# The second pair's first layer in two-level form, and its block sums spread over three earlier places

## The chip, the cores and the metric

The kernel runs on one core of a Trainium2 chip. Its time is the device time of one execution in microseconds (us). The core has five engines that run side by side, each with its own instruction queue that is worked off in order: TensorE (PE in the profile, with its weight loads as PEld), VectorE (DVE), ScalarE (ACT), GpSimd (POOL) and SyncE (SP), which here only issues DMAs. ScalarE and GpSimd issue some DMAs too. An instruction that waits on a semaphore holds all that stands behind it in its queue.

## The reference, cut to what matters

Four batches of 768 rows and 512 columns (8 heads of 64) go through a decayed linear attention in blocks, then through a Fourier mixing layer, a layer norm and an MLP:

```
attn_out = lightning attention of q, k, v with a decay per head
x    = attn_out as (4, 768, 512)
u    = x + real(fft over rows and columns of x)
un   = (u - mean(u)) / sqrt(var(u) + 1e-06)
out  = u + maximum(un @ w_ch1, 0) @ w_ch2
```

`w_ch1` is 512 x 2048 and `w_ch2` is 2048 x 512, all in float32. The MLP is what the change is about.

## The kernel before, in words

**Units of work.** The rows of a batch are cut into six tiles of 128 rows; a group is two of them, so that there are 12 groups of 256 rows. The first four groups (`PLAIN`) go through the MLP with ordinary matrix products (`mlp`), woven between the attention and the Fourier mixing of the four batches. The last eight (`LATE`) make four pairs, numbered 0 to 3, which are done at the end (`late`). For these the normalised rows were put into DRAM (`utd`), transposed, and so were the rows `u` (`ud`).

**Seven products in place of eight.** In a pair, both layers multiply blocks by a scheme that needs seven products of half-size blocks where the plain way needs eight; in exchange, sums and differences of the blocks of both operands are formed ahead (`combine_weights` makes those of the weights, once: `s1` to `s4` of `w_ch1` and `t1` to `t4` of `w_ch2`), and the results are added up from the accumulators. `PRODUCTS` lists the seven, 0 to 6, by their operand names. Two-level means that each of the seven is itself done by seven products of quarter blocks (`seven`), for which sums of the quarters are needed: three of them are read from DRAM (`load_three`), the fourth (the difference S3) takes the place of a quarter of the weight block itself.

**What the pairs do.** The second layer is two-level in all four pairs (`second_layer`, `deep_second`; matmuls on line 1048). The first layer is one-level in pairs 0 and 1 (`first_layer`, matmuls on line 893, 128 x 256) and two-level in pairs 2 and 3 (`deep_first`, matmuls on line 978, 128 x 128). `DEEP = 2` says so. The order of products in a two-level first layer is `FIRST = [0, 3, 4, 2, 1, 5, 6]`.

**Who makes the quarter sums.** Those of `w_ch2` (`keep_sums`, line 731, to DRAM as `td`) are made by GpSimd during pair 0's first layer, those of `w_ch1` (`keep_sums_w`, line 747, as `sd`) by GpSimd during pair 1's first layer: seven blocks of four sums each, 128 x 512, with the results written to DRAM through the SP queue. After that `place_sums_w` writes the seven S3 into the weight blocks (line 753).

**Order around the change.** The program is recorded once and a scheduler orders every engine's instructions when it is built, some of them pinned to the order of the text. In a second layer and a two-level first layer, `in_step` runs two neighbouring products alternately; the loads of the next product's sums (line 770, six buffers `tx`, three per product) and the sums of the activations stand in front of it. Each of the seven steps in a product is added into a PSUM accumulator, which VectorE or ScalarE reads (`read`, lines 1054 and 1056 in the second layer, 985 and 987 in the first) before the step after next adds to it again: the first, third, fifth and seventh step share one accumulator. The sums of the activations are made by VectorE: lines 872, 874 and 876 (`prepare_a`), 858 (`split`) and 950 (`part_sum`). The input rows of a pair come by `load_u` (line 759) into the buffer `ur`, of which there is one. The results of a pair lie in the tile `y2`, of which there is one too; it is stored by two SP DMAs (line 631) and two GpSimd scatter DMAs (line 633). GpSimd also adds `u` to the results (line 1062).

**The last batch's attention.** A batch is worked off in six chunks of 128 rows. In each, VectorE multiplies two tiles of scores by the decay (line 304) that TensorE made (line 300) and that it uses next (line 341); GpSimd makes `kd` (line 272) and the decayed state (line 324), and starts the gathers of mirrored rows (lines 448, 454 and 461).

Of the kernel before, what the change touches and what calls it, by code (L numbers as in the profile page):

```python
# [10 lines left out]
F32 = mybir.dt.float32  # L11
# [65 lines left out]
def kernel(  # L77
# [162 lines left out]
                yield 1.0  # L240


    xs, xn_, xd = {}, {}, {}

    def pair(t, hp):
# [45 lines left out]
    def attn_out(b, c, head):  # L291
        kT, qT, qs, kd, vt = ins.pop((b, c))
        last = c == NC - 1


        mm = nc.tensor.matmul
        pss = [psum_a([C, HP, C]) for _ in range(2)]
        for hp in range(HP):
            for hi in range(2):
                mm(pss[hi][:, hp, :], lhsT=kT[HD[hi], hp, :], rhs=qT[HD[hi], hp, :], start=True, stop=True)  # L300
        sc = []
        for hi in range(2):
# [12 lines left out]
        if not last:  # L315
            pu = psum_a([128, HP, D])
            for hp in range(HP):
                for hi in range(2):
                    h = 2 * hp + hi
                    mm(pu[HD[hi], hp, :], lhsT=kd[:, h, :], rhs=vt[:, h, :], start=True, stop=True)  # L320
            if c == 0:
                nc.vector.tensor_copy(s_new, pu)
            else:
                nc.gpsimd.tensor_tensor(s_new, s_old, spow.broadcast_to([128, HP, D]), op=ALU.mult)
                nc.vector.tensor_tensor(s_new, s_new, pu, op=ALU.add)
            if not padded:
                yield 0.9


        po = psum_a([128, HP, C])  # L330
        if c > 0:
            for hp in range(HP):
                for hi in range(2):
                    old, qh = (sd[:, hp, hi, :], qs[:, hp, :]) if padded else (s_old[HD[hi], hp, :], qs[HD[hi], hp, :])
                    mm(po[HD[hi], hp, :], lhsT=old, rhs=qh, start=(hp == 0), stop=False, skip_group_check=True)  # L335
        if padded and not last:
            for hi in range(2):
                nc.scalar.copy(sd[HD[hi], :, hi, :], st[HD[hi]])
        for hp in range(HP):
            for hi in (1, 0) if padded else (0, 1):  # L340
                mm(po[HD[hi], hp, :], lhsT=vt[:, 2 * hp + hi, :], rhs=sc[hi][:, hp, :],  # L341
                   start=(c == 0 and hp == 0), stop=(hp == HP - 1), skip_group_check=True)
        oT = new(at, [128, HP, C], "oT")
        nc.scalar.copy(oT, po)
        if b in TURNED:

            if c == 0:
                nc.scalar.copy(first, po[:, :, 0:1])
            elif c > 1:
                nc.scalar.copy(oTs[b][:, :, 0:1], po[:, :, 0:1])  # L350
        yield 2.0
        yield from head

        def turn(oT):
            px = psum_a([C, HP, 128])
            for hp in range(HP):
                nc.tensor.transpose(px[:, hp, :], oT[:, hp, :], ident)  # L357
            return px.rearrange("p h e -> p (h e)")

        def put(px, x, n=128):  # L360
            nc.scalar.copy(x[0:n, 0:HM], px[0:n, 0:HM])
            nc.scalar.copy(x[0:n, HM:DM], px[0:n, DM - 1:HM - 1:-1])

        def back(oT, x):
            put(turn(oT), x)

        if b not in TURNED:
            x = xn_[b, c] = new(xp, [C, DM], "x") if c < HC else new(xn, [C, DM], "xn")
            back(oT, x)
            if c == 0:  # L370
                xd[b] = (dram.tile([S - 256, DM], F32, name=f"xa{b}"), dram.tile([257, DM], F32, name=f"xb{b}"))
                nc.scalar.dma_start(xd[b][1][256:257], x[0:1])
            elif not last:
                nc.scalar.dma_start(xd[b][0][(c - 1) * C:c * C], x)
            if c >= NC - 2:
                nc.scalar.dma_start(xd[b][1][(c - NC + 2) * C:(c - NC + 3) * C], x)
            if c == NC - 2 and b - 1 not in LEADS:
                mirror_a(b)
            elif last:
                mirror_b(b)  # L380
            yield 1.7
            return


        if c == 2:
            eo[b] = new_eo()

        def mirrored(m, px):
            if m < HC:
                put(px, eo[b][HC - 1 - m][1][:, 1, 0:DM][0:BLK[HC - 1 - m]], BLK[HC - 1 - m])  # L390
            else:
                u = xs[b, HC + NC - 1 - m] = new(xp, [128, DM], "x")
                put(px, u)

        px = turn(oTs[b]) if c > 1 else None
        if c > 0:

            oTs[b] = new(fp, [128, DM + 4], "ds")[:, 0:DM].rearrange("p (h c) -> p h c", h=HP)
            tc.keep_in_program_order(nc.scalar.copy(oTs[b][:, :, C - 1:0:-1], po[:, :, 1:C]))
        if last:  # L400
            tc.keep_in_program_order(nc.scalar.copy(oTs[b][:, :, 0:1], first))
        if c > 1:
            mirrored(c - 1, px)
            yield 1.4
        if not last:
            x = xn_[b, c] = new(xp, [C, DM], "x") if c < HC else new(xn, [C, DM], "xn")
            back(oT, x)
            yield 1.7
        else:
            mirrored(c, turn(oTs[b]))  # L410
            for t in range(HC):
                xs[b, t] = xn_.pop((b, t))
            yield 1.4
# [317 lines left out]
            pin(nc.gpsimd.tensor_tensor(o, x, y, op=op))  # L731
            nc.sync.dma_start(s2.td[k][i], o)

    s2.sd = []

    def quarters_w(t):

        return [t[:, k, f:f + FH // 2] for f in (0, FH // 2) for k in range(2)]

    def keep_sums_w(k):  # L740

        pin = tc.keep_in_program_order
        A11, A12, A21, A22 = quarters_w(s2.A[PRODUCTS[k][0]])
        S3, S2, S1, S4 = [new(s2.yp, [128, FH // 2], "tx", bufs=6) for _ in range(4)]
        s2.sd.append([dram.tile([128, FH // 2], F32, name=f"sd{k}{i}") for i in range(4)])
        for i, o, x, y, op in ((3, S3, A11, A21, SUB), (1, S2, A22, S3, SUB), (0, S1, S2, A11, ADD), (2, S4, A12, S2, SUB)):
            pin(nc.gpsimd.tensor_tensor(o, x, y, op=op))
            nc.sync.dma_start(s2.sd[k][i], o)

    def place_sums_w():  # L750

        for k, (a, _) in enumerate(PRODUCTS):
            nc.sync.dma_start(quarters_w(s2.A[a])[2], s2.sd[k][3])

    def load_u(j, queue=nc.sync):

# [18 lines left out]
        pass  # L775

    PAIRS = len(LATE) // 2
    DEEP = 2
    pairs = [Pair() for _ in range(PAIRS)]
    for P_ in pairs:  # L780
        P_.pre_a, P_.pre_b, P_.pre_w = {}, {}, {}
# [104 lines left out]
    def first_layer(j):  # L886
# [24 lines left out]
        for i in range(HF):  # L911
# [14 lines left out]
            V.tensor_tensor(a22, two(Z), a22, op=ADD)  # L926
            V.tensor_scalar(a22, a22, 0.0, None, op0=ALU.max)
            last = (i, X, Z)
            if j < min(DEEP, 2) and i < len(PRODUCTS):
                if i == 0:  # L930
                    tc.keep_in_program_order(nc.gpsimd.tensor_copy(s2.begun, h["a11"][:, 0, 0, 0:1]))
                (keep_sums, keep_sums_w)[j](i)
            if i == HF - 3:
                load_x(j)
            if i == HF - 2:
# [4 lines left out]
        run(prepare_a(j, 0))  # L940
        finish(*last)
        run(prepare_a(j, 1))
        if j + 1 < PAIRS:
            load_u(j + 1)
        open_y(j)

    def part_sum(e, o, x, y, op):
# [17 lines left out]
    def deep_first(j, k):  # L965
# [15 lines left out]
        def read(ps, r, s, first):  # L981
# [7 lines left out]
            if k > 3 and done[r, s] == (1 if (r, s) == (0, 1) else 2):  # L989
                nc.scalar.activation(o, o, AF.Relu)  # L990

        yield from seven(mm, read)

        T, a11, a12, a21, a22 = (h[n] for n in ("s1", "a11", "a12", "s3", "a22"))
# [37 lines left out]
    def deep_second(j, k):  # L1032
# [18 lines left out]
        def read(ps, s, m, first):  # L1051
# [3 lines left out]
            else:  # L1055
                V.tensor_tensor(o, ps[:, 0:HM // 2], o, op=ADD)  # L1056

        yield from seven(mm, read)

        def add_u(o, y, k, m):  # L1060
# [19 lines left out]
        elif k == 3:  # L1080
            V.tensor_tensor(y22, y22, T, op=ADD)
            add_u(y21, y22, 1, 0)
            add_u(T, T, 0, 1)
            add_u(y22, y22, 1, 1)
        elif k == 4:
            V.tensor_tensor(y22, y22, y12, op=ADD)
            V.tensor_tensor(y12, y12, T, op=ADD)
        elif k == 5:
            store(*who[1][1], yt[:, 1, 1])
        else:  # L1090
            store(*who[0][1], yt[:, 0, 1])
            store(*who[1][0], yt[:, 1, 0])
            store(*who[0][0], yt[:, 0, 0])
# [54 lines left out]
                        del live[q]  # L1148

    def late():  # L1150
        for j in range(PAIRS):
            if j < DEEP:
                open_pair(j)
                if j == 0:
                    run(inputs(0))
                first_layer(j)
                if j + 1 < DEEP:
                    in_step(second_layer(j) + [(inputs(j + 1), iter(()))])
        in_step(second_layer(DEEP - 1) + [w for j in range(DEEP, PAIRS) for w in deep_pair(j)])


# [113 lines left out]
```

## Time and profile before

| | us |
|---|---|
| median of three runs | 793.12 |
| lowest and highest run | 791.16 and 796.66 |
| the profiled execution's own time | 794.64 |
| its span, from the first to the last instruction | 792.3 |
| TensorE busy in the span | 763.7 (96%) |
| weight loads | 648.6 (82%) |
| VectorE | 587.0 (74%) |
| ScalarE | 224.9 (28%) |
| GpSimd | 196.2 (25%) |

All instants below are us from the start of the span. The stages of the end, by the lines of TensorE's matmuls: pair 0's first layer from 427, its second layer from 472; pair 1's first layer from 518, its second layer from 564; pair 2 from 607 with a two-level first layer, pair 3 from 695. TensorE's busy time counts modelled ends, so that a busy row says that it was not waiting, not that it could go no faster. The granted TensorE clock was 0.994 of full speed in the mean.

### The profile page before, as it was taken

How to read it: one execution, taken by the hardware profiler on the slowest of the kernel's cores; microseconds unless marked ns; L12 is line 12 of the kernel's file. 1: busy time of each engine (PE TensorE's matmuls, PEld its weight loads, DVE VectorE, ACT ScalarE, POOL GpSimd, SP SyncE). 2: the span in 40 equal slices, each digit the busy share in tenths (PEclk: the TensorE clock that was granted, in tenths of full speed). 3: DMA queues.
4: the chain of work that ended last, by engine and by line, in shares of the span. 5: the costliest groups of instructions: out<-in, count | busy, mean ns of one | idle time of the engine just before them, and what ended most of it. 6: DMA issues, size and time to landing. Idle time of an engine off the chain costs nothing.

```text
span 792.3 us, 14623 instructions
## 1 busy us (share of the span) xinstructions
PE 763.7 (96%) x5616; PEld 648.6 (82%) x5616; DVE 587.0 (74%) x1148; ACT 224.9 (28%) x532; POOL 196.2 (25%) x198
## 2 busy tenths in 40 slices
PE   6889989999999899999999999999999999999996
PEld 5768776858675876868946889988999999999996
DVE  6899889675745482345698998769966699758983
ACT  3665443335531221421201221022211342024300
POOL 3213331011111020211003960279204001230012
PEclk9999999999999899999999999999999999999999
DMA  9979724238843138431243375345954555456442
GB/s 236 258 155 249 194 81 127 96 62 213 218 125 99 40 59 167 120 99 43 54 120 104 136 244 158 98 167 193 346 151 148 160 175 182 126 174 186 132 121 81
DMA packets 152331, 116.80 MB, mean 147 GB/s; under 512 B 113998, under 2 KB 113998, under 8 KB 152262
## 3 DMA queue, kind: packets, MB, share of 16 engines
q1 hardware_dynamic: 147120, 103.39, 46.7%
q0 software_dynamic: 2112, 6.69, 2.6%
q10 hardware_dynamic: 3030, 5.78, 2.0%
q8 instruction: 45, 0.74, 0.4%
q14 instruction: 24, 0.20, 0.1%
HBM read 83.58 MB, written 32.25 MB: 146 GB/s over the span
## 4 chain that ended last, share of the span: by engine, by line
PE 81%; DVE 9%; DMA 4%; issue 2%; ACT 1%; POOL 1%; POOLq 0%; SPq 0%; ACTq 0%
PE p L1048 21%; PE p L893 12%; PE p L978 11%; PE pm L658 10%; PE pm L644 10%; PE pa L525 3%; PE pa L300 3%; PE pa L341 3%; DMA x<-xb,ix 2%; PE pa L335 2%; PE pa L276 1%; PE pa L320 1%; PE pa L281 1%; PE pa L357 1%; DVE sc L304 1%
## 5 line engine op out<-in xcount | busy, mean ns | idle before, releaser
L644 PE MATMUL pm<-ut,w 128*128 128x256 f32 x512 | 118.4, 381 | 0.0
L658 PE MATMUL pm<-w,hr 128*128 128x512 f32 x256 | 115.3, 596 | 0.1
L644 PEld LDWEIGHTS pm<-ut,w 128*128 128x128 f32 x512 | 94.5, 190 | 13.6 <-issue 2.1
L658 PEld LDWEIGHTS pm<-w,hr 128*128 128x128 f32 x256 | 46.7, 190 | 50.3 <-issue 48.9
L1062 POOL TENSOR_TENSOR y<-y,u 128x512 f32<-128x512 f32 x12 | 18.9, 1572 | 199.1 <-DVE y L1071 156.7
L1048 PE MATMUL p<-tx,sx 128*128 128x128 f32 x416 | 54.9, 275 | 0.0
L1048 PEld LDWEIGHTS p<-tx,sx 128*128 128x128 f32 x416 | 50.6, 192 | 0.0
L272 POOL TENSOR_TENSOR kd<-k,decay 128x512 f32<-128x512 f32 x20 | 22.5, 1124 | 97.9 <-PE pa L320 51.6
L893 PE MATMUL p<-ur,w 128*128 128x256 f32 x192 | 46.7, 379 | 0.0
L1054 ACT COPY y<-p 128x128 f32<-128x128 f32 x48 | 12.8, 266 | 104.1 <-PE p L1048 103.1
L1056 DVE TENSOR_TENSOR y<-p,y 128x128 f32<-128x128 f32 x92 | 25.5, 285 | 22.5 <-PE p L1048 15.9
L893 PEld LDWEIGHTS p<-ur,w 128*128 128x128 f32 x192 | 36.4, 190 | 5.3 <-issue 0.5
L1048 PE MATMUL p<-w,ha 128*128 128x128 f32 x288 | 37.4, 275 | 0.0
L300 PEld LDWEIGHTS pa<-qT,kT 64*128 64x128 f32 x384 | 26.1, 193 | 13.0 <-ACT qT L283 7.8
L304 DVE TENSOR_TENSOR sc<-pa,decay 128x512 f32<-128x512 f32 x48 | 31.4, 682 | 6.6 <-PE pa L300 6.4
L1048 PEld LDWEIGHTS p<-w,ha 128*128 128x128 f32 x288 | 35.0, 192 | 0.2
L652 ACT ACTIVATE hr<-pm 128x256 f32<-128x256 f32 x44 | 16.7, 385 | 63.8 <-PE pm L644 63.6
L300 PE MATMUL pa<-qT,kT 64*128 64x128 f32 x384 | 30.7, 292 | 3.4 <-ACT qT L283 3.1
L558 POOL TENSOR_SCALAR ve<-mv 128x2 f32<-128x2 f32 x12 | 3.3, 278 | 121.8 <-DVE mv L555 121.8
L893 PE MATMUL p<-sx,w1s 128*128 128x256 f32 x128 | 32.9, 380 | 0.5 <-DVE sx L796 0.5
L341 PE MATMUL pa<-sc,v 128*64 128x128 f32 x384 | 29.9, 279 | 2.8 <-DVE sc L304 2.8
L987 DVE TENSOR_TENSOR ha<-p,ha 128x512 f32<-128x512 f32 x40 | 26.7, 684 | 6.5 <-PE p L978 6.3
(234 smaller groups left out, 1723.1 us busy)
## 6 DMA issues: line engine op xcount, KB each, us to landing
tx<-td SPq DMA_DIRECT2D x84, 256.0 KB, 2.9
raw<-in_moe_w_ch_dram SPq DMA_DIRECT2D x32, 512.0 KB, 4.8
tx<-sd SPq DMA_DIRECT2D x42, 256.0 KB, 2.8
sd<-tx SPq DMA_DIRECT2D x28, 256.0 KB, 2.0
k<-in_k_dram SPq DMA_DIRECT2D x24, 256.0 KB, 5.5
q<-in_q_dram SPq DMA_DIRECT2D x24, 256.0 KB, 5.1
v<-in_v_dram SPq DMA_DIRECT2D x24, 256.0 KB, 4.5
td<-tx SPq DMA_DIRECT2D x21, 256.0 KB, 2.0
```

The lines of the kernel that those rows point to most:

```text
L272: nc.gpsimd.tensor_tensor(kd, kt, kpow, op=ALU.mult)
L300: mm(pss[hi][:, hp, :], lhsT=kT[HD[hi], hp, :], rhs=qT[HD[hi], hp, :], start=True, stop=True)
L304: nc.vector.tensor_tensor(t, pss[hi], decay[:, hi::2, :], op=ALU.mult)
L341: mm(po[HD[hi], hp, :], lhsT=vt[:, 2 * hp + hi, :], rhs=sc[hi][:, hp, :], start=(c == 0 and hp == 0), stop=(hp == HP - 1), skip_group_chec ...
L525: mm = nc.tensor.matmul(ps[:, n, :], lhsT=piece(a, i, n), rhs=cs[0:rows, a, i in (2, 3), n, :], start=(a == 0), stop=(a == 1))
L644: nc.tensor.matmul(ps, lhsT=w1[:, c, 128 * fc:128 * fc + 128], rhs=ut[:, c, :], start=(c == 0), stop=(c == KO - 1))
L658: nc.tensor.matmul(ps, lhsT=hr[(fc - f0) // 4][:, fc % 4, 128 * i:128 * i + 128], rhs=w2[:, fc, :], start=(fc == f0), stop=(fc == f1 - 1))
L893: nc.tensor.matmul(ps, lhsT=s2.A[a][:, kt, 128 * i:128 * i + 128], rhs=U[b][:, kt, :], start=(first and kt == 0), stop=(kt == 1), skip_gro ...
L978: nc.tensor.matmul(ps[:, 128 * i:128 * i + 128], lhsT=ab[m][0][:, 128 * i:128 * i + 128], rhs=ab[m][1], start=(start and i == 0), stop=Tru ...
L987: V.tensor_tensor(o, p, o, op=ADD)
L1048: nc.tensor.matmul(ps[:, 0:HM // 2], lhsT=ab[m][0][i], rhs=ab[m][1][:, i, :], start=(start and i == 0), stop=(i == HF // 2 - 1), skip_grou ...
L1056: V.tensor_tensor(o, ps[:, 0:HM // 2], o, op=ADD)
```

## The change

`DEEP` goes from 2 to 1, so that pair 1's first layer is two-level as well. Its sums of `w_ch1` quarters must then be there before pair 1, and they are made by one new function, `block_sums`, in three places:

- for products 0, 1 and 5 by VectorE in chunks 1 to 4 of the last batch's attention, one of the twelve sums at each `next(early)`, in two buffers of the pool `ep`; all four results of a block go to DRAM by the GpSimd queue;
- for products 3 and 4 by GpSimd at the start of pair 0's second layer, in a spare `ur` buffer; S3 is formed in place in the weight block, the three others go to DRAM by the GpSimd queue;
- for products 2 and 6 by GpSimd at the start of pair 1's first layer, in a spare `y2` buffer; S3 in place, the three others go to DRAM by the SP queue.

`place_sums_w` now writes three S3 and runs in pair 0's second layer. The load of pair 1's rows (`load_u(1)`) moves from the end of pair 0's first layer to the fourth product of its second layer. The 28 sums of `keep_sums_w` and their DMAs in pair 1's first layer go.

```diff
+    def quarters_w(t):
+        return [t[:, k, f:f + DFF // 4] for f in (0, DFF // 4) for k in range(2)]
+    sums_of = {}
+    def block_sums(eng, queue, k, t, stage, inside):
+        Q11, Q12, Q21, Q22 = quarters_w(t)
+        d = sums_of[k] = [dram.tile([128, DFF // 4], F32, name=f"sd{k}{i}") for i in range(4)]
+        s1, s2_, s4, s3 = (stage[i] for i in range(4))
+        o = {3: Q21 if inside else s3, 1: s2_, 0: s1, 2: s4}
+        for i, x, y, op in ((3, Q11, Q21, ALU.subtract), (1, Q22, 3, ALU.subtract), (0, 1, Q11, ALU.add), (2, Q12, 1, ALU.subtract)):
+            x, y = (o[z] if isinstance(z, int) else z for z in (x, y))
+            tc.keep_in_program_order(eng.tensor_tensor(o[i], x, y, op=op))
+            if i < 3 or not inside:
+                queue.dma_start(d[i], o[i])
+            yield 1.0
+    def front_sums():
+        for k, a in ((0, w1[:, 0:2, 0:DFF // 2]), (1, w1[:, 2:4, 0:DFF // 2]), (5, w1[:, 2:4, DFF // 2:DFF])):
+            E, F = (new(ep, [128, DFF // 4], "e") for _ in range(2))
+            yield from block_sums(nc.vector, nc.gpsimd, k, a, (E, F, F, E), False)
+    early = front_sums()
...
+        sums = b == B - 1 and 0 < c < NC - 1
+        if sums:
+            next(early)
         po = psum_a([128, HP, C])
...
         nc.scalar.copy(oT, po)
+        if sums:
+            next(early)
...
+            if sums:
+                next(early)
             if c == NC - 2 and b - 1 not in LEADS:
...
-    def keep_sums_w(k):
...
-        for k, (a, _) in enumerate(PRODUCTS):
-            nc.sync.dma_start(quarters_w(s2.A[a])[2], s2.sd[k][3])
+        for k in (0, 1, 5):
+            nc.sync.dma_start(quarters_w(s2.A[PRODUCTS[k][0]])[2], s2.sd[k][3])
...
-    DEEP = 2
+    DEEP = 1
...
-            if j < min(DEEP, 2) and i < len(PRODUCTS):
+            if i < len(PRODUCTS):
...
-                (keep_sums, keep_sums_w)[j](i)
+                keep_sums(i)
...
         run(prepare_a(j, 1))
-        if j + 1 < PAIRS:
-            load_u(j + 1)
         open_y(j)
...
+        if j == DEEP and k < 2:
+            if k == 0:
+                P.spare = spare_y()
+            run(block_sums(nc.gpsimd, nc.sync, (2, 6)[k], s2.A[("s3", "s4")[k]], P.spare, True))
         yield from seven(mm, read)
...
+        if j < DEEP and k < 2:
+            if k == 0:
+                P.spare = spare_u()
+            run(block_sums(nc.gpsimd, nc.gpsimd, (3, 4)[k], s2.A[("s2", "s1")[k]], P.spare, True))
         yield from seven(mm, read)
...
             add_u(y22, y22, 1, 1)
+            if j < DEEP:
+                load_u(j + 1)
...
     def late():
-        for j in range(PAIRS):
-            if j < DEEP:
-                open_pair(j)
-                if j == 0:
-                    run(inputs(0))
-                first_layer(j)
-                if j + 1 < DEEP:
-                    in_step(second_layer(j) + [(inputs(j + 1), iter(()))])
+        open_pair(0)
+        run(inputs(0))
+        first_layer(0)
         in_step(second_layer(DEEP - 1) + [w for j in range(DEEP, PAIRS) for w in deep_pair(j)])
```

In this cut, the first `if` stands at the start of a product of `deep_first` and the second at the start of one of `deep_second`. In the program as built, TensorE's order is the same as before up to pair 0's last products; VectorE's is the same but for the twelve sums in the attention and for pair 1. In the SP queue, the two DMAs of `load_u(1)` stand between the first and the second of the three loads for pair 0's product 3 (counted from 0), and the six writes of the sums of products 2 and 6 stand among the loads of pair 1's products.

More of the change, by code (lines that the diff above doesn't have):

```diff
@@ L732, in keep_sums, with four, spare_u, spare_y @@
             nc.sync.dma_start(s2.td[k][i], o)
-    s2.sd = []
-    def quarters_w(t):
-        return [t[:, k, f:f + FH // 2] for f in (0, FH // 2) for k in range(2)]
-    def keep_sums_w(k):
[L742 to L748, printed above, removed]
+    s2.sd = sums_of
+    def four(t):
+        return [t[:, 512 * i:512 * i + 512] for i in range(4)]
+    def spare_u():
+        return four(new(s2.up, [128, 2, KO, G * 128], "ur").rearrange("p a b c -> p (a b c)"))
+    def spare_y():
+        return four(new(s2.yp, [128, 2, G, DM], "y2").rearrange("p a b c -> p (a b c)"))
     def place_sums_w():
-        for k, (a, _) in enumerate(PRODUCTS):
-            nc.sync.dma_start(quarters_w(s2.A[a])[2], s2.sd[k][3])
+        for k in (0, 1, 5):
+            nc.sync.dma_start(quarters_w(s2.A[PRODUCTS[k][0]])[2], s2.sd[k][3])
     def load_u(j, queue=nc.sync):
```

## The prediction

> **What bounds the kernel now.** I read the page's slices first, then the chain that ended last, then the stretches, and last the time order of single instructions where two engines meet. The slices (40 of 19.8 us each) show TensorE at eight or nine tenths from the second slice on. GpSimd is full only in slices 23 and 28, in the two one-level first layers, and there VectorE is at nine too.
>
> ```profile
> PE   6889989999999899999999999999999999999996
> ...
> DVE  6899889675745482345698998769966699758983
> ...
> POOL 3213331011111020211003960279204001230012
> ```
>
> The chain, in order of time (start, length, what), is TensorE alone from 427 to 780:
>
> ```profile
> 427.21 45.13 PE p L893 x208
> 472.34 0.67 PE p L1048 x6
> 473.01 1.79 PE p L893 x8
> 474.80 43.10 PE p L1048 x386
> 517.90 46.62 PE p L893 x216
> 564.52 0.67 PE p L1048 x6
> 565.19 1.79 PE p L893 x8
> 566.98 40.42 PE p L1048 x362
> ```
>
> So a matmul saved at the end is time saved, as long as nothing that feeds TensorE becomes late.
>
> **The gain.** Pair 1's first layer is 224 matmul records on line 893: 46.62 + 1.79 = 48.41 us, 0.216 each. In two-level form it is 7 products x 7 steps x 8 records = 392. Pair 2 has just this, without a gap:
>
> ```profile
> 612.76 38.41 PE p L978 x344
> ```
>
> 38.41 / 344 = 0.1117, and 392 x 0.1117 = 43.77. The gain is **4.64 us**. That the 28 GpSimd sums in pair 1's first layer go (of some 1.35 us each) is worth nothing by itself: TensorE was dense beside them.
>
> **The twelve sums in the attention.** VectorE gets 12 x 0.68 (line 872 has the same operands) = 8.2 us, GpSimd 12 DMA issues; a plain DMA from that queue does not occur before, the nearest row is the scatter on line 633 with 1.06 us of the engine and 3.0 from issue to landing. Between 304 and 347 VectorE has gaps of 8.3, 3.0, 3.0, 3.4, 2.6, 2.6 and 4.3 us, and GpSimd has gaps of 14.7 and 3 us. Most of it lies beside TensorE's work. The catch: with two buffers, a sum waits until an earlier one has landed in DRAM, and behind it in VectorE's queue stand the score products (line 304), which TensorE uses 0.1 us after they end (end 333.24, use from 333.37; 339.12 and 339.25). In chunk 2, the sum ending at 328.45 is written by 328.5 + 3.0 = 331.5, so the one that waits ends at 332.2 where the scores start at 332.03: 0.1 to 0.2 late. In chunk 3 the like count gives 338.0 against 337.91. I take **+0.2**; bounds 0 (landing in 2.0, as SP's writes of `sd`) and 2.5 (4.3, the slowest GpSimd gather's, which adds 1.3 in each of the two chunks). The GpSimd queue is through at 346.2, before the gather at 347.30.
>
> **Sums 3 and 4 in pair 0's second layer: the dear part.** GpSimd was idle there and seems free. VectorE is not:
>
> ```profile
> core 0: us, PE busy (x) PEld busy (x) DVE busy (x) ACT busy (x) POOL busy (x), PEclk, DMA share, GB/s
> 472.00:485.00 13.00, 13.00 (x109) 12.77 (x108) 12.71 (x25) 2.74 (x10) 0.00 (x0) 1.00 0.70 227
> ```
>
> 12.71 of 13 us, with GpSimd at 0.00. And the two hinder each other. Of these lines the first two and the last ran while GpSimd summed, the third while it was idle; the fourth is a read of PSUM that I come to below:
>
> ```profile
> 461.98 1.75 DVE L858 TENSOR_TENSOR ha<-ha 128x512 f32<-128x512 f32 x1
> ...
> 465.27 1.48 DVE L908 TENSOR_TENSOR hs<-ha,sv 128x256 f32<-128x256 f32 x1
> ...
> 468.61 0.68 DVE L858 TENSOR_TENSOR ha<-ha 128x512 f32<-128x512 f32 x1
> ...
> 479.64 0.28 DVE L1056 TENSOR_TENSOR t<-p,t 128x128 f32<-128x128 f32 x1
> ...
> 505.19 1.34 DVE L874 TENSOR_TENSOR sx<-sx,ha 128x512 f32<-128x512 f32 x1
> ```
>
> The same sum of two SBUF operands takes 0.68 alone and up to 1.75 beside GpSimd: up to 1.07 per GpSimd sum. The three GpSimd adds at 503.5 to 507.7 cost VectorE only 0.66 + 0.30, so 0.32 each. Those are the bounds. When: the first sum can start when its weight block is last used (470.5), the second when `ur` is free (473.96, where the load of line 759 got going). From there five sums and three DMA issues take 5 x 1.27 + 3 x 1.06 = 9.5, to 483.5. So six sums start before 482.00, which is when TensorE adds the seventh step of product 0 to an accumulator:
>
> ```profile
> 482.00 1.06 PE L1048 MATMUL p<-w,sx 128*128 128x128 f32 x8
> ```
>
> It may do so once VectorE has read the fifth step, which is the line at 479.64, done at 479.92: 2.1 us to spare. VectorE's queue ahead of that read has no gap from 470 on and is 15 operations on SBUF to 5 that read PSUM, so nearly all that it loses arrives there. Six sums cost 6 x 0.32 = 1.9 to 6 x 1.07 = 6.4; less 2.1 that is 0 to 4.3 us of TensorE standing still. I take the upper end, **+4.3**, because line 858 (two SBUF operands, 512 wide, in a queue without gaps) is the row most like this queue, while the adds at 503.5 met PSUM reads and gaps. The last two sums meet the like place in product 1 (read at 485.85, use at 488.25); with 0.6 us of VectorE's idle time between, that could bring the stage to 8 x 1.07 - 0.6 - 2.1 = 5.8, the stage's upper bound.
>
> The Trainium skill ("SBUF — State Buffer", Who interferes with whom) says that a VectorE operation with two SBUF inputs and a GpSimd operation that reads SBUF exclude each other for a whole instruction, the loser blocking fully. Taken at its word each sum may cost its whole 1.27 us, 7.6 for six, and 5.5 us of stall where I have 4.3; the rows show 0.32 to 1.07. The same page (the box on "DVE blocks DMA") warns that a GpSimd-issued DMA can be starved of descriptors by VectorE, which speaks against the 18 new DMAs; no run here shows that.
>
> **`load_u(1)`, moved.** It waits for the last of these DMAs: 473.96 + 7 x 1.27 + 5 x 1.06 + 3.0 = 491.2, and in SP's queue two loads for product 3 wait behind it. With its own 1 MB ahead (5.7 from issue to landing) the first of them lands at about 497.5, where TensorE wanted it at 497.19. Alone this costs 0.3; under a stall of 4.3 it is hidden, so I take **0**, with 3 as the other end if GpSimd is later by that much.
>
> **Sums 2 and 6 in pair 1's own first layer.** Instants of pair 2 in before, less 92.2, stand for pair 1. The spare `y2` is free when pair 0's stores have landed: GpSimd's last scatter at 520.1, one sum later for the inserted S3 (521.4), landing 3.0; SP's two stores behind it, landing 2.2 after 524.9: 527.1. Then six sums of 1.3 to 535.0, each followed by its SP write, and behind these the load for product 2 (fourth in `FIRST`): 535.5 + 2.8 = 538.3. Pair 2's third step of that product began at 629.57, so it is wanted at 537.4. **+0.9**. Bounds: 0 (landing 0.9 sooner) and 4.8 (each sum alternating with a VectorE sum, 1.95 in place of 1.27).
>
> The three writes of `place_sums_w` wait until 474.7 and SP's next loads were due at 476.84: nothing, and 0.5 if they landed late.
>
> **Sum.** 794.64 - 4.64 + 0.2 + 4.3 + 0 + 0.9 = 795.4 for a profiled execution. The profiled one of before was 1.5 above its median, so the median comes to **794**.
>
> **Rivals.**
> - *The gain comes through.* If a GpSimd sum costs VectorE 0.3 (as at 503.5), its 1.9 stays under the spare 2.1. 794.64 - 4.64 + 0.2 + 0 + 0.3 + 0.9 = 791.4, median **790**. For it: ScalarE reads some accumulators, and in pair 0's first layer VectorE kept up beside GpSimd. Against: there it had only 2.9 us of work for each 6 us; here 12.7 for 13.
> - *Slower.* GpSimd's in-order queue in pair 1 is the bound: the `y2` release, then six sums that alternate with VectorE's, hold SP's writes and with them all loads behind. From a sum of more than 1.15 us on, TensorE waits for product 2; at 1.95 it waits 4.8. With the upper 5.8 of the stage before: 794.64 - 4.64 + 0.2 + 5.8 + 4.8 = 800.8, median **799**; the front's upper bound brings 802. For it: GpSimd's adds at 598.12 and 671.16 took 1.72 and 2.19 beside VectorE. Against: VectorE has gaps of 1.5 to 3.3 us early in that stage.
> - *The change does nothing there.* Excluded as to the instructions (pair 1's steps are on the two-level line as built); a two-level layer that isn't dense is the second rival.
>
> **How the numbers follow.** Forecast 0.55 (791.5 to 797), gain comes through 0.25 (787.5 to 791.5), slower 0.20 (797 to 806). The range leaves out a tenth at either end: 788.5 to 801. Over 1% is 7.9 us, about what a measurement of this kernel can tell from no change: below 785.2 takes more than the whole gain, 0.03; above 801 the slower rival's upper half, 0.10; the rest, 0.87, lies within.
>
> **What would show it.** In the changed profile: some 392 records of the two-level line between pair 0's and pair 1's second layers at 0.11 each (gain); VectorE's sums of lines 872 to 876 at 1.3 and more between 470 and 490, and a gap in TensorE at the seventh step of product 0 or the fifth of product 1, released by VectorE (contention); a TensorE wait for a `tx` load in pair 1's fourth product (its own sums). TensorE without gaps from 427 to the end would prove me wrong, and so would gaps in the attention of a us or more.

## The result, and the profile after

The changed kernel is slower: 804.51 us in the median of six runs (798.94 to 808.71) against 793.69 us for the kernel before, measured beside it (791.16 to 797.78). The ratio is 1.0113, with a 95% interval from 1.0079 to 1.0147. The prediction was 794, with a range from 788.5 to 801. The profiled execution took 803.61 us, with a span of 801.7 (before: 794.64 and 792.3).

These are the slices of the changed kernel's page, 40 of 20 us each.

```profile
PE   6888999999999999999999996998999999999996
...
DVE  6899889675846482555798999658997599758983
...
POOL 3223331011111010421005974253013200330012
PEclk9999999999999999999999998999999999999999
```

Before, TensorE was at eight or nine from the second slice on. Now the 25th (481 to 501 us) is at six: there GpSimd is at four, where it was at nought before, VectorE is at nine, and the granted clock falls to eight. The chain that ended last, which carried the reading of before, is no help after: it ends in the last store and covers 0% of the span. So the time order of TensorE's instructions is read, for the rows that waited. These are all the waits of TensorE in the changed kernel between 318 and the end but two that it has before too (start, length, what, in brackets the idle time just before and what ended it).

```profile
334.60 1.09 PE L370 MATMUL pa<-sc,v 128*64 128x128 f32 x16 [0.96 <-DVE sc L331]
...
341.79 1.09 PE L370 MATMUL pa<-sc,v 128*64 128x128 f32 x16 [1.20 <-DVE sc L331]
...
477.07 1.13 PE L924 MATMUL p<-sx,w 128*128 128x256 f32 x4 [0.65 <-DVE ha L957]
...
491.74 2.08 PE L1081 MATMUL p<-w,sx 128*128 128x128 f32 x8 [6.17 <-DVE t L1089]
...
552.20 2.02 PE L1007 MATMUL p<-sx,tx 128*128 128x128 f32 x16 [2.87 <-DMA tx<-sd]
```

Line numbers have moved by 27 to 33: L331 and L370 are the score products and their use (304 and 341 before), L924 the one-level first layer (893), L1081 the second layer (1048), L1089 its read (1056), L1007 the two-level first layer (978), L257 and L259 the new sums and their DMAs. The five rows stand in the three places where the sums went: the attention, pair 0's second layer, pair 1's own first layer. The dear one is the fourth, the seventh step of product 0, which began at 482.00 before.

These are stretches of the changed kernel around it (busy time of each engine and its instructions, the granted clock, DMA).

```profile
core 0: us, PE busy (x) PEld busy (x) DVE busy (x) ACT busy (x) POOL busy (x), PEclk, DMA share, GB/s
475.00:485.00 10.00, 9.35 (x76) 8.80 (x75) 9.89 (x15) 1.68 (x6) 7.39 (x8) 1.00 0.79 265
485.00:491.70 6.70, 0.56 (x6) 0.37 (x4) 6.70 (x5) 0.27 (x1) 5.31 (x6) 0.80 0.54 183
491.70:496.50 4.80, 4.76 (x25) 4.76 (x26) 4.70 (x8) 0.53 (x2) 0.00 (x0) 0.57 0.64 207
```

In the middle row VectorE is busy for all 6.70 us, and only five of its instructions fall into it, beside 5.31 us of GpSimd; TensorE stands. In the last row TensorE is busy again, but at a clock of 0.57.

**Where the 10 us are.** To compare executions free of what varies at their start, I take instants of TensorE: the last transposes ahead of the last batch's chunks (298.58 before), the first dependent step of pair 0's first layer (427.21), the first steps of pair 1 and pair 2, the last step of all (784.11). Differences between them, in us, of the profiled executions, with the medians of all runs. The kernel before was measured again beside each group: 794.75 beside e1 to e4, 795.88 beside e5 to e8; ratios are to it, that of the changed kernel to the 793.69 above.

| kernel | front | pair 0 | pair 1 | whole | median | ratio to before (95%) |
|---|---|---|---|---|---|---|
| before | 128.63 | 180.02 for both | | 485.53 | | |
| changed | 130.96 | 97.14 | 90.65 | 495.63 | 804.51 | 1.0113 (1.0079 to 1.0147) |
| e1_memset | 130.81 | 87.85 | 92.10 | 487.64 | 794.70 | 1.0000 (0.9974 to 1.0026) |
| e2_vector | 130.98 | 90.42 | 92.12 | 490.40 | 799.15 | 1.0051 (1.0024 to 1.0078) |
| e3_half_writes | 130.85 | 97.17 | 88.34 | 493.24 | 802.12 | 1.0099 (1.0067 to 1.0131) |
| e4_front_sp | 129.30 | 97.91 | 90.77 | 494.86 | 805.65 | 1.0124 (1.0075 to 1.0172) |
| e5_four_early | 130.90 | 91.89 | 90.22 | 489.89 | 800.20 | 1.0085 (1.0050 to 1.0121) |
| e6_six_early | 130.95 | 95.03 | 93.68 | 496.54 | 800.98 | 1.0096 (1.0053 to 1.0140) |
| e7_vector_then_gpsimd | 129.18 | 89.83 | 87.82 | 483.71 | 791.73 | 0.9961 (0.9931 to 0.9992) |
| e8_vector_both | 129.25 | 88.74 | 88.39 | 483.26 | 789.90 | 0.9938 (0.9907 to 0.9969) |

Pair 1 to pair 2 without a wait is 87.55 (pair 2 to pair 3 in before), pair 0's two layers without a wait are 87.85 (e1_memset, where TensorE doesn't wait there). From pair 2 to the end it is 176.88 in every kernel. So the change of the whole, 10.10, is: front +2.33, pair 0 +9.29, pair 1 +3.10 of waits and 87.85 + 87.55 - 180.02 = -4.62 of gain.

### The profile page after: what moved, and what is told of

Its sections match the earlier page's. It is cut to its first block, busy times and chain, and to the rows that moved or that the text cites. A ratio compares the mean times of both kernels' runs of the same rounds, so it can differ in the third digit from the quotient of the medians.

```text
span 801.7 us, 14997 instructions
## 1 busy us (share of the span) xinstructions
PE 760.2 (95%) x5784; PEld 650.1 (81%) x5784; DVE 604.8 (75%) x1151; ACT 231.9 (29%) x532; POOL 198.8 (25%) x213
## 5 line engine op out<-in xcount | busy, mean ns | idle before, releaser
L1081 PE MATMUL p<-tx,sx 128*128 128x128 f32 x400 | 52.8, 275 | 0.0
L1081 PEld LDWEIGHTS p<-tx,sx 128*128 128x128 f32 x400 | 48.7, 192 | 0.0
L1016 DVE TENSOR_TENSOR ha<-p,ha 128x512 f32<-128x512 f32 x60 | 40.1, 686 | 9.9 <-PE p L1007 9.7
L1089 DVE TENSOR_TENSOR y<-p,y 128x128 f32<-128x128 f32 x92 | 25.6, 286 | 19.1 <-PE p L1081 12.2
L1081 PE MATMUL p<-w,ha 128*128 128x128 f32 x288 | 38.2, 279 | 0.0
L1007 PE MATMUL p<-sx,tx 128*128 128x128 f32 x264 | 34.0, 275 | 2.9 <-DMA tx<-sd 2.9
L1016 DVE TENSOR_TENSOR hs<-p,hs 128x512 f32<-128x512 f32 x39 | 26.2, 684 | 13.2 <-PE p L1007 13.2
L1081 PEld LDWEIGHTS p<-w,ha 128*128 128x128 f32 x288 | 35.7, 196 | 0.1
L331 DVE TENSOR_TENSOR sc<-pa,decay 128x512 f32<-128x512 f32 x48 | 31.4, 682 | 5.3 <-PE pa L327 5.0
L370 PE MATMUL pa<-sc,v 128*64 128x128 f32 x384 | 29.8, 279 | 5.7 <-DVE sc L331 5.7
L1007 PEld LDWEIGHTS p<-sx,tx 128*128 128x128 f32 x264 | 31.6, 192 | 3.0 <-issue 3.0
```

The lines of the kernel that those rows point to most:

```text
L1007: nc.tensor.matmul(ps[:, 128 * i:128 * i + 128], lhsT=ab[m][0][:, 128 * i:128 * i + 128], rhs=ab[m][1], start=(start and i == 0), stop=Tru ...
L1016: V.tensor_tensor(o, p, o, op=ADD)
L1081: nc.tensor.matmul(ps[:, 0:HM // 2], lhsT=ab[m][0][i], rhs=ab[m][1][:, i, :], start=(start and i == 0), stop=(i == HF // 2 - 1), skip_grou ...
```

## The experiments

The kernels e1 to e4 each change one thing in the changed kernel; e5 and e6 change how many sums come early; e7 and e8 put cures together.

**e1_memset: GpSimd's eight sums without the reading.** Eight memsets of the same tiles stand in their place; the sums of products 3 and 4 are left out.

```diff
-            run(block_sums(nc.gpsimd, nc.gpsimd, (3, 4)[k], ...))
+            run(block_sums(None, nc.gpsimd, (3, 4)[k], ...))
...
-            tc.keep_in_program_order(eng.tensor_tensor(o[i], x, y, op=op))
+            tc.keep_in_program_order(eng.tensor_tensor(o[i], x, y, op=op) if eng else nc.gpsimd.memset(o[i], 0.0))
```

> The changed kernel, with the eight GpSimd sums in pair 0's second layer replaced by GpSimd memsets of the same 128x512 tiles (the sums of products 3 and 4 are left out; queue, positions and DMA issues stay). Theory A (each sum keeps VectorE from reading its second SBUF operand): VectorE's operations between 472 and 491 return to 0.68 and 1.22, the gap of 6.2 us at TensorE's seventh step of product 0 goes, and with it the slow clock behind it (2.0): 0.8 + 6.4 + 2.0 = 9.3 us less, 804.5 to about 795.2. Theory B (the stall comes from GpSimd's DMA issues or its queue being late, not from the reading): the six DMA issues are still there, the gap stays above 4 us, less than 3 us gained.

The median is 794.70, 9.8 under the changed kernel. Rows of its time order, one of GpSimd, two of VectorE, one of TensorE:

```profile
478.75 0.55 POOL L257 MEMSET ur<- 128x512 f32 x1
...
482.09 1.22 DVE L979 TENSOR_TENSOR ha<-hs,ha 128x1024 f32<-128x1024 f32 x1
483.23 0.28 DVE L1089 TENSOR_TENSOR t<-p,t 128x128 f32<-128x128 f32 x1
...
485.31 1.06 PE L1081 MATMUL p<-w,sx 128*128 128x128 f32 x8
```

The line of 128x1024 takes 1.22, where beside GpSimd's sums it took 2.75. The seventh step (last row) follows without a wait, and the pair takes 87.85. GpSimd's queue, its six DMA issues and their places are as they were, so neither they nor their landings made the stall: theory A holds. A memset is also shorter than a sum (0.55 for 1.27), so this alone doesn't tell reading from mere length; the rows of VectorE do: its operations with two SBUF inputs have their undisturbed lengths though they overlap the memsets. One row is an exception, with one input: the ReLU at 478.87 took 0.57 beside a memset, 0.29 alone.

**e2_vector: the same eight sums by VectorE.**

```diff
-            run(block_sums(nc.gpsimd, nc.gpsimd, (3, 4)[k], ...))
+            run(block_sums(nc.vector, nc.gpsimd, (3, 4)[k], ...))
```

> The changed kernel, with the eight sums in pair 0's second layer given to VectorE itself; the writes stay in GpSimd's queue. Theory A: a sum now costs VectorE its own 0.60 in a row in place of the 1.17 that a GpSimd sum took from it; 8 x 0.60 = 4.8, less 2.1 of slack and 0.6 of idle time is a stall of at most 2.1, and less where the order lets a later operation step back; no slow clock behind a stall that short. Gain 9.3 - (0 to 2.1), so 795.2 to 797.5. Theory B (VectorE is full there, whoever sums): the work is added to VectorE's queue in full and the stall stays at 5 or more, 803 to 805.

The median is 799.15, 5.4 under the changed kernel. Pair 0 takes 90.42, 2.57 over the undisturbed 87.85 where GpSimd's sums cost 9.29. The busy engine does the work cheaper than its idle neighbour. But 2.0 of the difference is the slow clock (below), which did not come here, and VectorE's order is another: the line of 128x1024 (1.13 of its queue), which stood before the read of the fifth step, stands behind it. So this run doesn't give the price of a sum alone. The loss is over the 2.1 that theory A allowed, and VectorE's and TensorE's time order names a term that it lacked:

```profile
482.98 0.69 DVE L257 TENSOR_TENSOR ur<-w1s 128x512 f32<-128x512 f32 x1 [0.94 <-DMA sd<-ur]
...
490.16 1.16 PE L1081 MATMUL p<-w,sx 128*128 128x128 f32 x8 [2.31 <-DVE y L1089]
```

Block 4's sums take block 3's places in the spare tile, and in VectorE's queue they wait for the writes to land: 0.94 + 0.45 + 0.72 = 2.1 us, with the accumulator reads behind them. The miss of the time as a whole has a second cause: pair 1's wait of 2.71 was followed by a slow clock here, which cost 1.7 (see the end); the changed kernel had none there.

**e3_half_writes: block 6's writes by GpSimd.**

```diff
-            run(block_sums(nc.gpsimd, nc.sync, (2, 6)[k], ...))
+            run(block_sums(nc.gpsimd, (nc.sync, nc.gpsimd)[k], (2, 6)[k], ...))
```

> The changed kernel, with the three writes of block 6's sums in pair 1's own first layer issued by GpSimd in place of SP. Theory A (SP, in order, stood before these three writes from 544.9 to 548.7 with the load for product 2 behind): the load is issued 3.8 earlier, TensorE's wait of 2.9 at 552 for tx goes, 804.5 to about 801.6. Theory B (the load waits for the landing of the sd tile itself, or for the tx buffers): the wait stays above 2, no more than 1 us gained.

The median is 802.12, and pair 1 takes 88.34 instead of 90.65: 2.3 less. First the SP queue of the changed kernel, then that of this one (start, time until the group's last issue, what):

```profile
544.86 3.79 SPq L259 DMA_DIRECT2D sd<-y  x3
548.75 8.49 SPq L801 DMA_DIRECT2D tx<-sd  x8
```

```profile
544.59 11.03 SPq L801 DMA_DIRECT2D tx<-sd  x9
...
551.43 1.16 PE L1007 MATMUL p<-sx,tx 128*128 128x128 f32 x8 [0.35 <-DVE hs L1016]
```

SP stood before the writes of block 6 until 548.75, with the load for product 2 behind them. Without them it goes on at 544.59, and the wait for `tx` is gone. What takes its place is 0.35 of VectorE. Theory A holds.

**e4_front_sp: the attention's writes by SP.**

```diff
-            yield from block_sums(nc.vector, nc.gpsimd, k, a, (E, F, F, E), False)
+            yield from block_sums(nc.vector, nc.sync, k, a, (E, F, F, E), False)
```

> The changed kernel, with the twelve writes of the attention's sums issued by SP in place of GpSimd. Theory A (the front is late by the 3.3 us from GpSimd's issue to landing with two buffers): SP's writes land in 2.0 to 2.2, the waits of VectorE's sums at 332.65, 337.80 and 339.46 shrink by 1.1 each, and the shift of 2.5 at the start of the late part falls to 0.5 or less; 804.5 to about 802.4. Theory B (VectorE's own added work of 12 x 0.68 makes the front late, or SP's loads of k and q are now late behind the writes): the shift stays at 2 or more.

The front shrinks from 130.96 to 129.30, so that 0.67 is left of 2.33. One of TensorE's two waits is gone; the other stays. From VectorE's and TensorE's time order:

```profile
342.16 0.69 DVE L257 TENSOR_TENSOR e<-w,e 128x512 f32<-128x512 f32 x1 [2.47 <-DMA sd<-e]
...
345.46 1.09 PE L370 MATMUL pa<-sc,v 128*64 128x128 f32 x16 [0.76 <-DVE sc L331]
```

The wait for the writes is the cause, as theory A says, and not VectorE's added work, which is the same here. But it isn't cured as A expected: 2.0 to 2.2 was only the fastest landing. Of SP's twelve the trace shows seven landings, 2.0 to 5.1 after the issue, 2.8 in the median; GpSimd's at the same place took 2.3 to 4.8, 3.2 in the median (ten each in e1, e2, e3, e5 and e6). So SP's writes landed little sooner, and the slowest no sooner. In chunk 2 the write came in time; the one issued at 336.96, just ahead of a load of `k`, took the 5.1, and the sum of the first row waited for it until 342.16. The gain of 1.7 isn't seen in the median (805.65, six runs). In the profiled execution 0.77 of it went to a longer slow clock in pair 0; beyond that, the median's scatter is larger than the effect, and the trace alone carries this verdict.

**e5_four_early and e6_six_early: the price by the count.** In both the last sums move behind GpSimd's add of product 1, so that they can't start early, and pair 1's load of `ur` goes to GpSimd's queue behind them. For e5:

```diff
-        if j < DEEP and k < 2:
-            if k == 0:
-                P.spare = spare_u()
-            run(block_sums(nc.gpsimd, nc.gpsimd, (3, 4)[k], ...))
+        if j < DEEP and k == 0:
+            P.spare = spare_u()
+            run(block_sums(nc.gpsimd, nc.gpsimd, 3, s2.A["s2"], P.spare, True))
...
             add_u(y11, y11, 0, 0)
+            if j < DEEP:
+                run(block_sums(nc.gpsimd, nc.gpsimd, 4, s2.A["s1"], P.spare, True))
...
-                load_u(j + 1)
+                load_u(j + 1, nc.gpsimd)
```

In e6, block 4's first two sums stay at the start of product 1, and two move.

> The changed kernel with only block 3's four GpSimd sums at the start of pair 0's second layer; block 4's four stand in GpSimd's queue behind its add of product 1 (at 491 in before), and the load of the next input behind them on the same queue. VectorE's order is as in the changed kernel. Theory A (a price per sum, paid ahead of one read that has 2.1 to spare): 4 x 1.17 - 2.1 = 2.6 of TensorE's time lost up to the seventh step of product 0 in place of 7.3, little or no slow clock behind it, up to 1 for the late four, which meet a VectorE with gaps: 9.3 less becomes 2.6 to 3.6, so 798 to 799. Theory B (only the first sums hurt, by holding the end of the first layer, or the stall has a fixed size): the gap at that step stays above 5.

> As the run with four early sums, but with six ahead of that add (block 3's four and block 4's first two) and two behind it: the count that the prediction took. Theory A (price 1.17, no other cause): 6 x 1.17 - 2.1 = 4.9 lost up to the seventh step, the slow clock (2) behind it as the wait is over 3, so 6.9 of the 9.3: about 802. Theory B (the price of the prediction is right and the two more sums were the whole error): 6 x 1.07 - 2.1 = 4.3. Either way between four and eight early sums; if the loss is not in line with the count, the price per sum falls.

The seventh step of TensorE in e5, then a second wait in e5, and in the next view the seventh step in e6:

```profile
483.06 1.16 PE L1081 MATMUL p<-w,sx 128*128 128x128 f32 x8 [0.99 <-DVE t L1089]
...
501.92 1.16 PE L1081 MATMUL p<-tx,ha 128*128 128x128 f32 x8 [1.62 <-DVE t L1089]
```

```profile
488.34 2.08 PE L1081 MATMUL p<-w,sx 128*128 128x128 f32 x8 [3.09 <-DVE t L1089]
```

Before, this step came 482.00 - 427.21 = 54.79 after the first dependent step of pair 0. In e5 that one was at 426.22, so the step is 483.06 - 481.01 = 2.05 late; in e6 (429.40) it is 488.34 - 484.19 = 4.15 late; in the changed kernel (429.69) 491.74 - 484.48 = 7.26. With the 2.1 of slack that is 4.15 for four sums, 6.25 for six, 9.36 for eight: 1.04 a sum for the first six, and 1.56 each for the last two. The loss goes by the count, and theory B of e5 falls. VectorE's own rows give the same without the slack: what its operations beside these sums took over their undisturbed lengths comes to 4.24 in e5, 6.34 in e6 and 9.41 in the changed kernel. The price of 1.17 that I took for these runs was the mean over unequal sums: e5's expected 2.6 and e6's 4.9 were both too high by it. The late four of e5 were not nearly free, as expected, but cost 91.89 - 87.85 - 2.05 = 2.0: VectorE's gaps there are 0.6 at a time, and operations of 0.68 took up to 2.05. e5's time came as 800.20 where 798 to 799 was expected; e6's time of 802 came as 800.98, though its profiled execution had the slow clock twice.

**e7_vector_then_gpsimd and e8_vector_both: the cures together.** Block 3 by VectorE at product 0, block 4 behind product 1 by GpSimd (e7) or by VectorE (e8), with e3's and e4's edits.

```diff
-            run(block_sums(nc.gpsimd, nc.gpsimd, 3, s2.A["s2"], P.spare, True))
+            run(block_sums(nc.vector, nc.gpsimd, 3, s2.A["s2"], P.spare, True))
...
-                run(block_sums(nc.gpsimd, nc.gpsimd, 4, s2.A["s1"], P.spare, True))
+                run(block_sums(nc.vector, nc.gpsimd, 4, s2.A["s1"], P.spare, True))
```

(The second of these two edits, against e5, is e8's alone.)

> Three cures together: block 3's sums by VectorE at the start of pair 0's second layer, block 4's by GpSimd behind the add of product 1, with the next input's load on the same queue; block 6's writes by GpSimd; the attention's writes by SP. By the parts: second layer 4 x 0.60 - 2.1 = 0.3, with 0 to 1.5 for the late four, in place of 9.3; own stage 0.8 in place of 3.1; front 0.7 in place of 2.3. 804.5 - 8.3 - 2.3 - 1.6 = 792.3, that is 1 to 2 below the kernel before. If a new wait stands behind one of them (the input's load too late for the sums of pair 1, wanted 5 before its start), 795 or more.

> The same, but block 4's sums also by VectorE, behind product 1, where VectorE has about a third of its time idle. Theory A: 8 x 0.60, four of them under 2.1 of slack and four in gaps: 0.3 to 1 in the second layer; 791.5 to 792.5, and no operation of VectorE there over 1.3 (512 wide over 0.7). Theory B (VectorE's queue, not the lock, decides): the four late sums delay the accumulator reads by 2.4, and it is no better than the run with GpSimd's.

Both are faster than the kernel before: 791.73 (ratio 0.9961, interval 0.9931 to 0.9992) and 789.90 (0.9938, interval 0.9907 to 0.9969), e7 only just. TensorE's waits in e8 from the second layer on:

```profile
496.03 1.16 PE L1081 MATMUL p<-w,sx 128*128 128x128 f32 x8 [0.61 <-DVE y L1089]
...
540.47 1.16 PE L1007 MATMUL p<-sx,tx 128*128 128x128 f32 x8 [0.40 <-DVE hs L1016]
```

In e8 pair 0 takes 88.74, 0.89 over the undisturbed; in e7 89.83, where the late four by GpSimd cost the same 2.0 as in e5 (at most 1.5 was expected). So block 3's four by VectorE cost nothing: ahead of the read there were 2.1 to spare for 4 x 0.60, and the scheduler put the 128x1024 line (1.13 of the queue) behind the read. The gain of the two-level layer is now there: by the traces, the whole is 1.82 (e7) and 2.27 (e8) under before. The medians are 4.2 and 6.0 under the one beside them; part of that is clock, since the mean granted clock was 0.9945 and 0.9955 in the median of their runs and 0.993 in that of before (0.0025 of the time is 2.0 us), and the rest is open. Neither is free of the front's rest (0.62 in e8). e8 came below the 791.5 to 792.5 expected, and one of its conditions failed: a sum of VectorE took 1.56 (at 492.41), beside GpSimd's add of 1.65.

## Why the prediction was wrong, point by point

The sum said 794.64 - 4.64 + 0.2 + 4.3 + 0 + 0.9 = 795.4. By the traces it should have been 794.64 - 4.62 + 2.3 + 9.3 + 0 + 3.1 = 804.7, and the profiled execution took 803.61 (its tail behind TensorE's last step was shorter by 0.85, and less time lay outside the span).

**What bounds the kernel, and the gain: right.** TensorE bounds the late part, and the two-level layer takes 4.62 less, as against 4.64. It came whole, and was lost elsewhere.

**Sums 3 and 4: the mechanism and the price right, the count wrong; this is the step that failed.** The prediction said up to 1.07 a sum, six sums before the read that matters, 2.1 of slack, 4.3 of stall. With six sums held to six, the stall is 4.15 (e6); the price, taken from one row, held in the mean, since the six rows lose between 0.68 and 1.43. But nothing held them. The count ended at 482.00, the instant at which TensorE wanted the accumulator in the trace of *before*. As VectorE fell behind, the read at 479.64 moved to 491.40 (2.48 of it is the later start of pair 0), and the last two sums came ahead of it too, at 1.56 each. So the stall was 7.26 in place of 4.3, and with the 2.0 of slow clock behind it the term was 9.3. From VectorE's and GpSimd's time order in the changed kernel:

```profile
478.51 1.84 DVE L938 TENSOR_TENSOR hs<-sv,ha 128x256 f32<-128x256 f32 x1
...
484.89 1.75 DVE L907 TENSOR_TENSOR sx<-ha,sx 128x512 f32<-128x512 f32 x1
486.56 2.24 DVE L903 TENSOR_TENSOR sx<-hs 128x512 f32<-128x512 f32 x1
488.73 2.75 DVE L979 TENSOR_TENSOR ha<-hs,ha 128x1024 f32<-128x1024 f32 x1
491.40 0.28 DVE L1089 TENSOR_TENSOR t<-p,t 128x128 f32<-128x128 f32 x1
...
484.49 1.60 POOL L257 TENSOR_TENSOR ur<-w1s 128x512 f32<-128x512 f32 x1
...
486.97 1.27 POOL L257 TENSOR_TENSOR ur<-ur,w1s 128x512 f32<-128x512 f32 x1
...
489.12 1.27 POOL L257 TENSOR_TENSOR ur<-w1s,ur 128x512 f32<-128x512 f32 x1
```

VectorE's rows take 0.42, 0.68, 0.68, 1.22 and 0.28 undisturbed. Each of the four long ones ends about its undisturbed length after the end of a GpSimd sum, so that it loses about the time from its own start to that end. This is why the last two sums were dearer: beside the sixth, the operation began 0.40 behind the sum (484.89 against 484.49) and lost 1.07; beside the last two it began 0.4 ahead (486.56 against 486.97, 488.73 against 489.12), was held all the same, and lost 1.56 and 1.53. The prediction's separate upper bound for eight (5.8) had the count but took the price of the first six, and 0.6 of idle time that was not there.

The Trainium skill ("SBUF — State Buffer", SBUF: two separate sides), which the prediction weighed against the rows, says that the loser blocks for a whole instruction. Taken at its word, a whole sum of 1.27 each; the first six cost 1.04, and the last two more than one sum each. Another section of that page (Who interferes with whom) says that a GpSimd instruction that only writes SBUF doesn't hinder a two-input VectorE operation; e1's rows agree (0.68 and 1.22 beside memsets).

**The stall's own consequence: not in the prediction at all.** Behind the 6.17 us of waiting, the next 24 matmuls took 491.74 to 496.46, 4.72 in place of 24 x 0.1117 = 2.68. That is 2.04 us more, at a granted clock of 0.50 to 0.63. It would have belonged to the forecast too: a stall of 4.3 was put down at 4.3, and e6, with a wait of 3.09, lost 3.0 behind it:

```profile
core 0: us, PE busy (x), PEclk, DMA share, GB/s
...
490.00:492.00 2.00, 2.00 (x11) 0.50 0.00 0
...
496.00:500.00 4.00, 4.00 (x39) 1.00 0.65 196
```

Eleven matmuls in 2 us at a clock of 0.50 in the first row, 39 in 4 us in the second. The profile of before had the price, in the 14th slice of its page (granted clock at eight), from which nothing was taken. There TensorE waits 2.19 us, and 12 and 16 matmuls of the kind that take 2.23 and 2.79 at 369.58 and 372.09 take 4.01 and 4.40, at a clock of 0.51. TensorE in before, in order of time and then by stretch:

```profile
259.84 4.01 PE L525 MATMUL pa<-cs,fe 65*128 65x193 f32 x12 [2.19 <-DVE fe L484]
263.64 4.40 PE L525 MATMUL pa<-cs,fo 128*128 128x193 f32 x16
...
369.58 2.23 PE L525 MATMUL pa<-cs,fe 65*128 65x193 f32 x12 [0.96 <-DVE fe L484]
```

```profile
core 0: us, PE busy (x), PEclk, DMA share, GB/s
...
259.90:266.90 7.00, 7.00 (x23) 0.51 0.10 37
```

The Trainium skill ("TensorE: Matmul & The Clock Gate", What's actually happening) says that the array's clock falls to a half after an idle window of about 3.4 us, and that the windows run freely. Here it followed a shorter wait.

**The twelve sums in the attention: a term mis-sized.** The mechanism was the one named (two buffers, a sum that waits for a landing, the score products behind it). I took 0.2 with the upper bound 2.5 for a landing of 4.3; it was 2.33. I had put a landing of 3.0 behind the end of the sum. A buffer came free 3.6 to 4.5 after its sum had ended (335.87 to 339.46, 328.64 to 332.65, 333.34 to 337.80): the issue comes 0.3 after the end, and the landing took 3.3 to 4.2 from there. A gap in the attention of a us or more, which the prediction named as a sign of being wrong, came with the wait of 1.20. e4 shows that the writes do it.

**`load_u(1)`, moved: right.** It was issued at 493.09, and no row of TensorE or VectorE waits for it. The larger stall stood ahead of it; whether that hid the 0.3 isn't shown.

**Sums 2 and 6: a term mis-sized, inside its bounds.** 0.9 was taken of 0 to 4.8, and it was 3.1. In order: the spare tile was free 0.4 later in the stage than worked out; the six sums took 9.0 in place of 7.9, the last three 1.60 to 1.72 beside VectorE; the load landed 3.45 behind its issue in place of 2.8. The place was as named, TensorE's wait for `tx` in pair 1's fourth product. e3 shows that it was SP standing before the last three writes.

**The rivals and the range.** "The gain comes through" is excluded by pair 0's loss. "Slower" had its place in pair 1, with 4.8, and its upper case of 800.8 to 802; what decided was the other place, pair 0. The range left out its upper half. Three terms came above the value taken, two inside their bounds (2.33 of 2.5, 3.1 of 4.8) and one above its bound (9.3 for 5.8). GpSimd and VectorE hindering each other stands behind pair 0 and pair 1, DMAs that land later than taken behind the front and pair 1; with all three long at once the time lay above the range.

**What stays open.** What decides whether the clock falls behind a wait isn't shown, only what it costs (last section). In pair 1 it came in e1, e2 and e6 and not in the changed kernel, e4 and e5. It goes with the spread of the runs: in every kernel the longer executions are, with few exceptions, those with the lower mean granted clock (before: 789.79 at 0.998 and 800.90 at 0.987; changed: 798.94 at 0.994 and 808.71 at 0.987).

## What to carry to other kernels

GpSimd isn't free because it is idle in the profile, if VectorE beside it is full: GpSimd's sums took 1.04 us each from VectorE in the mean of six and 1.56 beyond, more than the 0.6 that VectorE needs to do them itself. When a stall is worked out by counting what comes ahead of a deadline, count again with the deadline moved by the stall, until the count stops growing; and for a wait of TensorE of some 2 us or more, put a slow clock into the range, with nothing to 3.4 us for it. A write's buffer is free only after the wait for its producer, the issues ahead of it in the queue and the landing, and in an in-order queue the loads behind it wait as long.

## What the runs showed of the hardware

- **The clock behind a wait of TensorE.** By the granted clock of the ten traces, behind the start-up and up to TensorE's last step, the clock falls to a half for 3.41 or 6.83 us at a time. What is lost is about half of the part of it in which TensorE works: behind the wait of 6.17 (changed) it was at a half from 489.00 to 495.83, TensorE began again at 491.74, and 4.09 / 2 = 2.04; in e4 it began later within the like wait, 491.53 to 498.36 with TensorE from 492.71, and cost 2.8; 3.05 and 3.09 (e6) cost 2.9 and 3.0; 2.69 (e1) and 2.71 (e2) cost 1.7, with a stretch that began only behind the wait. Nothing was lost at 2.87 (changed) and 2.99 (e4), nor in pairs 0 and 1 at up to 2.44 (0.99, 1.62, 1.70, 2.31, 2.44). But the wait for `fe` at about 260 was followed by it with 2.19 (before), 2.21 (e7), 2.25 (e3), 2.35 (e4), 2.45 (changed) and 2.60 (e8), and not with 1.81 (e5), 2.17 (e6), 2.23 (e2) and 2.44 (e1). So between 2.2 and 3.0 the length of the wait doesn't decide. The window of 3.4 us in the Trainium skill's section named above is longer than these waits, and the two lengths of the slow stretch are one and two such windows.
- **A VectorE operation with one SBUF input is hit too.** The ReLU of 128x256 in place (`tensor_scalar`, L937 and L958), 0.29 alone, took 1.35 and 0.94 beside GpSimd's sums in the changed kernel. The prediction took its price from operations with two SBUF operands.
- **GpSimd's plain DMA.** 0.54 to 0.68 us of the engine to issue 256 KB (the prediction's row, a scatter, had 1.06), 0.3 behind the sum that it writes, and in the attention a landing of 2.3 to 4.8, 3.2 in the median; in pairs 0 and 1 up to 5.7 (e3).
- **The start of an execution.** The same transposes, up to which the kernels' work is the same, came at 295.3 to 301.3 us in the ten profiled executions. Most of this is the slow clock before them: none in e2 and e5 (295.66 and 295.32), one of 3.41 us in the changed kernel (298.73), 6.83 in all in before, e1, e3, e6, e7 and e8 (298.29 to 299.70), 10.24 in e4 (301.33). A difference of some us between two single spans can be all from before that; distances between instants inside the trace don't have it.
